# Last token group: one VectorE instruction moved behind the next tile's sum, and a third one moved to the second layer

## The chip, the core and the metric

The kernel runs on one core of one Trainium2 chip. The core has a matrix engine (TensorE, in the profile PE, with its weight loads as PEld), VectorE (DVE), ScalarE (ACT), GpSimd (POOL) and SyncE (SP, which here issues most of the transfers). The engines run side by side. Each takes its own instructions in order, and waits for others by semaphores. The metric is the device time of one execution in microseconds, less is better. Single executions are compared by their profile, kernels by the median of several runs.

## The reference

Two blocks follow one another: a gated linear attention (B = 4, H = 8 heads, S = 768 steps, 48 columns each), and a mixture of four two-layer networks over its output.

```python
for t in range(S):
    state = alpha[:, :, t, :, None] * state + einsum('bhd,bhe->bhde', k[:, :, t], v[:, :, t])
    y[:, :, t] = einsum('bhd,bhde->bhe', q[:, :, t], state)
x = y.transpose(0, 2, 1, 3).reshape(3072, 384)
p = domain_probs / (domain_probs.sum(-1, keepdims=True) + 1e-09)
for e in range(4):
    h = maximum(x @ w1[e], 0.0)                 # 3072 x 1024
    out += p[:, e:e + 1] * (h @ w2[e])          # 3072 x 384
```

## The kernel before, in words

**Tiling.** The sequence is cut into 24 units of 128 tokens (6 chunks of 4 batches). They form seven groups, `gi` = 0 to 6: the first and the last have 2 units (256 tokens), the others 4 (512 tokens). `LAST` is 6. For each group and each expert `e`, `up` makes the first layer, 8 tiles of hidden columns (`fc` = 0 to 7, each 128 hidden columns by the group's tokens), and `down` makes the second. Groups 5 and 6 take turns: (5, 0), (6, 0), (5, 1), (6, 1) and so on, so that they share weights. Attention for a later group runs between the matrix products of earlier ones: `deal` gives its steps due times from fixed costs, and `advance` emits the steps that are due. Attention is over before group 5 begins.

**Three parts.** A float32 operand is written as three fp32r parts: top, low and dif, in the text also top, L and D. The products of the parts then run on TensorE in the fast format. In the first layer a tile has six products into a PSUM buffer `one` and three into a buffer `two`. These and the second layer's sums `ops0`, `ops1` share four PSUM buffers (tag "g").

**A tile's way (groups 2 to 6, where `split2` holds).** ScalarE copies `one` to `t` with a factor (L538). VectorE adds `two` to `t` (L540). Then `hidden_parts`, a generator, makes the hidden tile's parts: ScalarE the top part with the ReLU (L563), VectorE the low part L as max(t, 0) - top (L565), and VectorE the D part from top and L (`make_dif`, L573). `hidden_parts` makes D only for the first half of the tokens. The other half goes into the queue `later`, which `down` empties, one piece at every fifth product (`n % 5 == 4`). `t` has two buffers.

**Order by hand.** Everything is emitted in program order, and each engine keeps that order. `up` appends the generator of tile k to `finish`, and runs it to its end after the products of tile k+1 have been emitted and before tile k+1's own copy and add. So VectorE's order is add(k), L(k), D(k), add(k+1), and ScalarE's is t(k), top(k), t(k+1). After the last tile of a stage (`fc` = 7) its generator is run at once.

**Second layer.** `down` takes two slots (units) at a time. A pass has 48 products: parts 0 and 1 (top and low) of `fc` 0 to 5 for both slots (n = 0 to 23), parts 0 and 1 of `fc` 6 and 7 (n = 24 to 31), and part 2 (D) of all `fc`, for the first slot n = 32 to 39, for the second n = 40 to 47. `add_up` adds a finished sum into `acc` on VectorE (L641; in the last group the tile's name is QT), with `p_fine` for `ops0` after n = 29 (first slot) and n = 31 (second), with `p_all` for `ops1` after n = 39 and n = 47. For expert 0 the first of them is a copy on ScalarE (L639). A group of four units has two passes, and the second reuses the PSUM buffers of the first. A group of two has one pass.

Of the kernel before, what the change touches and what calls it, by code (L numbers as in the profile page):

```python
# [20 lines left out]
def kernel(  # L21
# [49 lines left out]
    NT = B * P  # L71
# [11 lines left out]
    n = np.arange(QUAD)[None, :]  # L83
# [30 lines left out]
    LAST = len(groups) - 1  # L114
# [22 lines left out]
    finish = deque()  # L137
# [4 lines left out]
    later = deque()  # L142
# [91 lines left out]
    def background():  # L234


        for piece in list(splitting):
            if next(piece, splitting) is splitting:
                splitting.remove(piece)
        if making and len(splitting) < 4:  # L240
            splitting.append(making.popleft())
            next(splitting[-1])
# [225 lines left out]
    def x_part(gi, part, kc):  # L468
        n = len(groups[gi]) * P
        if gi < LAST:  # L470
            return xTs[gi][:, part, kc, :n]
        t, i = divmod(part * KC + kc, NP * P // n)
        return xTs[gi][t].rearrange("p a n -> p (a n)")[:, i * n:(i + 1) * n]
# [20 lines left out]
    def up(gi, e, fc, slots=None):  # L494
        n = len(groups[gi]) * P
        lo, hi = (slots.start * P, slots.stop * P) if slots else (0, n)
        begins, ends = lo == 0, hi == n
        c, f = divmod(fc, FPQ)
        i = first_piece(gi, e) + c
        if fc == 0 and begins:  # L500
            for k in range(NQ):
                hidden[k] = hid.tile([P, 3, FPQ, NT], F32R, name="hT", bufs=NQ)
        if fc in ((0, 2) if gi == 1 else (0,)) and begins and not split2(gi, e):
            half = range(fc, fc + 2) if gi == 1 else range(NQ)
            for k in half:
                load_piece(1, (gi * E + e) * NQ + k, beside=True)
        if makes[0](gi, e) and ends and fc in SPLIT_AT[e in (0, E - 1)]:
            k = SPLIT_AT[e in (0, E - 1)].index(fc)
            making.append(split_piece(0, (gi * E + e) * NQ + k))
        if gi == 0 and ends and e + 1 < E and fc == (0 if e == 0 else FCH // 2):  # L510
            for k in range(NQ):
                load_piece(0, (e + 1) * NQ + k)
        col = slice(f * P, (f + 1) * P)
        if split1(gi, e):
            w = wt[0][i].rearrange("p t (c f) -> p t c f", f=QF)[:, :, :, col]
        else:
            w = wt[0][i].rearrange("p (c f) -> p c f", f=QF)[:, :, col]
        parts = [hidden[c][:, part, f, lo:hi] for part in range(3)]
        whole = parts[2].bitcast(F32)
        one = ps.tile([P, NT], F32, name="one", tag="g", bufs=4)[:, :hi - lo]  # L520
        if not split1(gi, e):
            for kc in range(KC):
                nc.tensor.matmul(one, lhsT=w[:, kc], rhs=xraws[gi][:, kc, lo:hi],  # L523
                                 start=(kc == 0), stop=(kc == KC - 1))
            nc.scalar.activation(out=whole, in_=one, func=ACT.Relu)
        else:
            two = ps.tile([P, NT], F32, name="two", tag="g", bufs=4)[:, :n]
            for out, terms in ((one, (1, 0)), (two, (2,))):
                for part in terms:
                    for kc in range(KC):  # L530
                        nc.tensor.matmul(out, lhsT=w[:, part, kc], rhs=x_part(gi, part, kc),  # L531
                                         start=(part == terms[0] and kc == 0),
                                         stop=(part == terms[-1] and kc == KC - 1))
            while finish:
                for _ in finish.popleft():
                    pass
            t = work.tile([P, NT], F32, name="t")[:, :n]
            nc.scalar.activation(out=t, in_=one, func=ACT.Copy, scale=FINE)  # L538
            if split2(gi, e):
                nc.vector.tensor_add(t, t, two)  # L540
                finish.append(hidden_parts(t, parts))
            else:
                nc.vector.tensor_add(whole, t, two)  # L543
                finish.append(rectified(whole))
        while finish and fc == FCH - 1:
            for _ in finish.popleft():
                pass
        background()
        if f == FPQ - 1 and ends:
            if gi == 0:  # L550
                for k in range(AHEAD if i == E * NQ - 1 else 0):
                    load_piece(0, i + 1 + k)
            elif gi != LAST - 1:
                del wt[0][i]
                load_piece(0, i + AHEAD)
            while late:
                load_piece(1, late.popleft())
            while stores:
                stores.popleft()()

    def hidden_parts(x, parts):
        top, low, dif = parts
        nc.scalar.activation(out=top, in_=x, func=ACT.Relu, scale=TRIM)  # L563
        yield
        nc.vector.scalar_tensor_tensor(out=low, in0=x, scalar=0.0, in1=top.bitcast(F32),  # L565
                                       op0=ALU.max, op1=ALU.subtract)

        n = x.shape[-1]
        make_dif(*(part[:, :n // 2] for part in parts))
        later.append([part[:, n // 2:] for part in parts])  # L570

    def make_dif(top, low, dif):
        nc.vector.scalar_tensor_tensor(out=dif, in0=top.bitcast(F32), scalar=1 / 4096.0,  # L573
                                       in1=low.bitcast(F32), op0=ALU.mult, op1=ALU.subtract)

    def rectified(t):
        nc.scalar.activation(out=t, in_=t, func=ACT.Relu)
        yield

    def down(gi, e, slots, between):  # L580


        first = first_piece(gi, e)
        halves_ = split2(gi, e)
        if slots[0] == 0 and makes[1](gi, e):
            making.extend(split_piece(1, first + k) for k in range(NQ))
        if slots[0] == 0 and makes[0](gi, e) and 0 < e < E - 1:
            making.extend(split_piece(0, first + k) for k in range(2, NQ))
        sums = [[ps.tile([P, DM], F32, name=f"ops{j}", tag="g", bufs=4)
                 for j in range(2 if halves_ else 1)] for _ in slots]  # L590

        kinds = [((0, 1), range(FCH - 2)), ((0, 1), range(FCH - 2, FCH)), ((2,), range(FCH))]
        steps = [(part, i, fc) for parts, tiles in (kinds if halves_ else [((3,), range(FCH))])
                 for part in parts for i in range(len(slots)) for fc in tiles]
        for n, (part, i, fc) in enumerate(steps):
            c, f = divmod(fc, FPQ)
            h = hidden[c][:, :, f, slots[i] * P:(slots[i] + 1) * P]
            advance(cost(1, gi, e) / FCH / (3 if halves_ else 1))
            while between and n >= between[0][0] * len(steps):
                between.popleft()[1]()  # L600
            if n == len(steps) // 2:
                background()
            if later and n % 5 == 4:
                make_dif(*later.popleft())
            if halves_:
                w = wt[1][first + c].rearrange("p t (c d) -> p t c d", d=DM)[:, part, f]
                nc.tensor.matmul(sums[i][part // 2], lhsT=h[:, part], rhs=w,  # L607
                                 start=(fc == 0 and part != 1), stop=(fc == FCH - 1 and part != 0))
            else:
                w = wt[1][first + c].rearrange("p (c d) -> p c d", d=DM)[:, f]  # L610
                nc.tensor.matmul(sums[i][0], lhsT=h[:, 2].bitcast(F32), rhs=w,  # L611
                                 start=(fc == 0), stop=(fc == FCH - 1))
            if part >= 1 and fc == FCH - 1:
                add_up(gi, e, slots[i], part // 2, sums[i][part // 2 if halves_ else 0])
        while between:
            between.popleft()[1]()
        background()
        if slots[-1] == len(groups[gi]) - 1 and gi != LAST - 1:
            while makes[1](gi, e) and (making or splitting):
                background()  # L620

            for c in range(NQ):
                del wt[1][first + c]
                if c < NQ // 2 or gi == LAST:
                    load_piece(1, first + NQ + c)
                else:
                    late.append(first + NQ + c)
# [68 lines left out]
    with tc.manual_schedule():  # L696
# [48 lines left out]
        for (gi, e), after in zip(tasks, [*tasks[1:], (None, None)]):  # L745
# [6 lines left out]
            for k, slots in enumerate(turns):  # L752

                between = deque()
                if after[1] == 0:
                    for step, at in enumerate((0.0, 0.52, 0.62, 0.72)):
                        at = at * len(turns) - k
# [33 lines left out]
```

## Time and profile before

| | us |
|---|---|
| median of 9 runs (1083.57 to 1085.19) | 1084.7 |
| the profiled execution, its own time | 1083.78 |
| its span in the profile | 1082.0 |
| PE busy | 1057.0 (98%) |
| PEld busy | 899.0 (83%) |
| DVE busy | 779.3 (72%) |
| ACT busy | 563.8 (52%) |
| POOL busy | 32.8 (3%) |

The page's times are of one execution. "L607 PE MATMUL ops<-w,hT" is an instruction of line 607 on PE that writes `ops` and reads `w` and `hT`; "x6" is a count. In a timeline the first column is the start in us and the second the length. What stands in brackets is how long the engine sat idle before it, and what ended that. In the chain that ended last, the second column is the time that the piece took on the chain. TensorE's clock was granted in full in nearly every slice, 0.998 in the mean.

### The profile page before, as it was taken

How to read it: one execution, taken by the hardware profiler on the slowest of the kernel's cores; microseconds unless marked ns; L12 is line 12 of the kernel's file. 1: busy time of each engine (PE TensorE's matmuls, PEld its weight loads, DVE VectorE, ACT ScalarE, POOL GpSimd, SP SyncE). 2: the span in 40 equal slices, each digit the busy share in tenths (PEclk: the TensorE clock that was granted, in tenths of full speed). 3: DMA queues.
4: the chain of work that ended last, by engine and by line, in shares of the span. 5: the costliest groups of instructions: out<-in, count | busy, mean ns of one | idle time of the engine just before them, and what ended most of it. 6: DMA issues, size and time to landing. Idle time of an engine off the chain costs nothing.

```text
span 1082.0 us, 21627 instructions
## 1 busy us (share of the span) xinstructions
PE 1057.0 (98%) x8460; PEld 899.0 (83%) x8460; DVE 779.3 (72%) x1743; ACT 563.8 (52%) x1202; POOL 32.8 (3%) x71
## 2 busy tenths in 40 slices
PE   8889899999999999999999999999999999999998
PEld 8766677686776798898898898898988989898987
DVE  5578777647567869778878777986787965756565
ACT  5786776674746555436546436565464442323232
POOL 2000000000000100000000000000000000000000
PEclk9999999999999999999999999999999999999999
DMA  8597689886696967757759559577594444453530
GB/s 123 156 329 229 213 267 374 297 307 237 220 320 217 407 201 268 283 169 294 269 167 353 216 172 361 182 254 273 147 348 190 176 191 175 175 186 164 206 160 30
DMA packets 158838, 251.67 MB, mean 233 GB/s; under 512 B 120112, under 2 KB 135344, under 8 KB 136208
## 3 DMA queue, kind: packets, MB, share of 16 engines
q1 hardware_dynamic: 149600, 208.82, 56.0%
q0 software_dynamic: 5760, 41.29, 9.7%
q8 instruction: 67, 1.10, 0.4%
q10 hardware_dynamic: 3376, 0.17, 0.3%
q14 instruction: 35, 0.29, 0.1%
HBM read 207.79 MB, written 42.47 MB: 231 GB/s over the span
## 4 chain that ended last, share of the span: by engine, by line
PE 77%; DVE 9%; ACT 7%; DMA 4%; issue 2%; SPq 1%; ACTq 0%; DVEq 0%
PE ops L607 25%; PE one L531 19%; PE two L531 9%; PE ops L611 9%; PE sc L333 5%; PE yps L425 3%; PE tp L265 2%; ACT qb L307 2%; DVE t L540 2%; DVE hT L565 2%; PE one L523 2%; ACT hT L563 2%; PE sps L454 1%; PE far L388 1%; DMA w<-kept 1%
## 5 line engine op out<-in xcount | busy, mean ns | idle before, releaser
L607 PE MATMUL ops<-w,hT 128*128 128x384 f32 x1728 | 318.5, 340 | 1.9 <-DVE acc L641 1.4
L607 PEld LDWEIGHTS ops<-w,hT 128*128 128x128 f32 x1728 | 299.2, 188 | 7.4 <-DVE acc L641 2.7
L531 PE MATMUL one<-xT,w 128*128 128x512 f32 x960 | 253.9, 400 | 1.1 <-DMA w<-kept 0.9
L531 PEld LDWEIGHTS one<-xT,w 128*128 128x128 f32 x960 | 175.8, 188 | 42.6 <-issue 2.4
L538 ACT ACTIVATE t<-one 128x512 f32<-128x512 f32 (+1 forms) x192 | 106.0, 552 | 162.7 <-PE one L531 146.5
L307 ACT COPY qb<-QT 64x256 f32<-64x256 f32 x336 | 136.5, 406 | 70.0 <-DVE QT L288 35.5
L563 ACT ACTIVATE hT<-t 128x512 fp32r<-128x512 f32 (+1 forms) x160 | 94.3, 590 | 122.3 <-DVE t L540 121.2
L565 DVE SCALAR_TENSOR_TENSOR hT<-t,hT 128x512 fp32r<-128x512 f32 (+1 forms) x160 | 102.2, 638 | 75.5 <-ACT hT L563 74.1
L531 PE MATMUL two<-xT,w 128*128 128x512 f32 x480 | 136.3, 392 | 0.0
L611 PE MATMUL ops<-hT 128*128 128x384 f32 x384 | 134.4, 493 | 0.0
L573 DVE SCALAR_TENSOR_TENSOR hT<-hT 128x256 fp32r<-128x256 f32 (+1 forms) x320 | 117.4, 395 | 5.5
L540 DVE TENSOR_TENSOR t<-t,two 128x512 f32<-128x512 f32 (+1 forms) x160 | 100.6, 629 | 23.7 <-PE two L531 13.2
L531 PEld LDWEIGHTS two<-xT,w 128*128 128x128 f32 x480 | 90.2, 188 | 19.9
L611 PEld LDWEIGHTS ops<-hT 128*128 128x128 f32 x384 | 69.5, 191 | 40.0 <-issue 0.8
L343 DVE COPY_PREDICATED near<-masks,sc 128x256 f32<-128x256 uint8 x144 | 77.0, 535 | 18.0 <-PE sc L333 14.9
L314 DVE TENSOR_TENSOR QT<-QT,dec 128x256 f32<-128x256 f32 x144 | 60.6, 421 | 32.6 <-ACT qb L307 32.2
L333 PEld LDWEIGHTS sc<-qb,KT 128*64 128x64 f32 x2304 | 72.8, 138 | 9.2 <-issue 7.1
L333 PE MATMUL sc<-qb,KT 128*64 128x64 f32 x2304 | 77.0, 224 | 0.2 <-ACT qb L307 0.2
L641 DVE SCALAR_TENSOR_TENSOR acc<-ops,p_all,acc 128x384 f32<-128x384 f32 x82 | 49.4, 612 | 29.2 <-PE ops L607 13.8
L325 ACT COPY KT<-KT 128x256 f32<-128x256 f32 x144 | 59.8, 415 | 3.1
L326 DVE TENSOR_TENSOR KT<-KT,dec 128x256 f32<-128x256 f32 x144 | 60.2, 418 | 1.5 <-PE tp L265 1.3
L543 DVE TENSOR_TENSOR hT<-t,two 128x512 f32<-128x512 f32 x32 | 22.0, 687 | 35.6 <-ACT t L538 25.3
(88 smaller groups left out, 970.7 us busy)
## 6 DMA issues: line engine op xcount, KB each, us to landing
w<-kept SPq DMA_DIRECT2D x144, 1152.0 KB
kept<-w POOLq DMA_DIRECT2D x32, 1152.0 KB, 7.6
hT<-in_moe_w_dram SPq DMA_DIRECT2D x32, 384.0 KB
w<-in_moe_w_dram SPq DMA_DIRECT2D x48, 128.0 KB
ra<-in_alpha_dram SPq DMA_DIRECT2D x23, 192.0 KB
rk<-in_k_dram SPq DMA_DIRECT2D x23, 192.0 KB
rq<-in_q_dram SPq DMA_DIRECT2D x23, 192.0 KB
out_dram<-acc POOLq DMA_DIRECT2D x18, 192.0 KB, 5.9
```

What stands on the lines that cost most here:

```text
L307: nc.scalar.copy(out=qb[rows, :, i, :].rearrange("p a (b r) -> p a b r", r=m), in_=qv[rows])
L314: nc.vector.tensor_mul(qv, qv, spread(dv[:, :, :, 0], m))
L333: nc.tensor.matmul(out[HALF * s:HALF * (s + 1), 2 * p:2 * p + 2, :], lhsT=KTs[li][:, p, HALF * s:HALF * (s + 1)], rhs=qbs[li][:, p, :, QUA ...
L343: nc.vector.copy_predicated(near.rearrange("p a (b two r) -> p a b two r", two=2, r=m)[:, :, :, 1, :], mk.unsqueeze(1).broadcast_to([P, H, ...
L531: nc.tensor.matmul(out, lhsT=w[:, part, kc], rhs=x_part(gi, part, kc), start=(part == terms[0] and kc == 0), stop=(part == terms[-1] and k ...
L538: nc.scalar.activation(out=t, in_=one, func=ACT.Copy, scale=FINE)
L540: nc.vector.tensor_add(t, t, two)
L563: nc.scalar.activation(out=top, in_=x, func=ACT.Relu, scale=TRIM)
L565: nc.vector.scalar_tensor_tensor(out=low, in0=x, scalar=0.0, in1=top.bitcast(F32), op0=ALU.max, op1=ALU.subtract)
L573: nc.vector.scalar_tensor_tensor(out=dif, in0=top.bitcast(F32), scalar=1 / 4096.0, in1=low.bitcast(F32), op0=ALU.mult, op1=ALU.subtract)
L607: nc.tensor.matmul(sums[i][part // 2], lhsT=h[:, part], rhs=w, start=(fc == 0 and part != 1), stop=(fc == FCH - 1 and part != 0))
L611: nc.tensor.matmul(sums[i][0], lhsT=h[:, 2].bitcast(F32), rhs=w, start=(fc == 0), stop=(fc == FCH - 1))
```

## The change

Three edits, all in order and place; each product, part and sum stays.

- In the last group, `finish`'s generator is only run by its first step (the top part) before the next tile's copy. Its second step (L) is run after that tile's add. In the other groups all is as before.
- `hidden_parts` makes no D in the first layer if the tile is narrower than 512 tokens, which is the last group. All 256 tokens of a tile go into `later` as one piece, so a pass has eight pieces of 128x256 where eight of 128x128 were left.
- `down` takes a piece from `later` at every fourth product (`n % 4 == 3`), in all groups that have pieces, 2 to 6: at n = 3, 7, ... 31, where it was n = 4, 9, ... 39.

```diff
-            while finish:
-                for _ in finish.popleft():
+            ends_first = gi < LAST
+            for steps in finish:
+                for _ in steps if ends_first else [next(steps)]:
                     pass
+            ahead = [] if ends_first else list(finish)
+            finish.clear()
             t = work.tile([P, NT], F32, name="t")[:, :n]
             nc.scalar.activation(out=t, in_=one, func=ACT.Copy, scale=FINE)
             if split2(gi, e):
                 nc.vector.tensor_add(t, t, two)
+                for steps in ahead:
+                    next(steps, None)
                 finish.append(hidden_parts(t, parts))
...
         n = x.shape[-1]
-        make_dif(*(part[:, :n // 2] for part in parts))
-        later.append([part[:, n // 2:] for part in parts])
+        at = n // 2 if n == NT else 0
+        if at:
+            make_dif(*(part[:, :at] for part in parts))
+        later.append([part[:, at:] for part in parts])
...
-            if later and n % 5 == 4:
+            if later and n % 4 == 3:
                 make_dif(*later.popleft())
```

## The prediction, made before the changed kernel was run

> **What bounds the kernel now.** I read the page's busy shares first, then the chain that ended last over 990 to 1082 us, then the timeline of the stage that the change names, then the waits.
>
> ```profile
> PE 1057.0 (98%) x8460; PEld 899.0 (83%) x8460; DVE 779.3 (72%) x1743; ACT 563.8 (52%) x1202; POOL 32.8 (3%) x71
> ```
>
> TensorE is the bound as an average: after 140 us nearly every slice is full. But the chain leaves PE in one kind of place, the first layer of the last group (tiles of 128x256). Its periods repeat like this one (start, length, what):
>
> ```profile
> 1013.73 0.02 issue
> 1013.75 0.04 DVE hT L573
> 1013.78 0.17 issue
> 1013.96 0.42 DVE t L540
> 1014.38 0.02 issue
> 1014.41 0.43 ACT hT L563
> 1014.83 0.02 issue
> 1014.86 0.44 DVE hT L565
> ```
>
> One period runs from add to add, 1012.39 to 1013.96: 1.57 us. VectorE adds (L540), ScalarE makes the top part (L563), VectorE makes L (L565) and then D (L573), and only behind these, in VectorE's order, comes the next add. PE's side of it, and ScalarE's, in the timeline:
>
> ```profile
> 1012.02 0.98 PE L531 MATMUL one<-KT,w 128*128 128x256 f32 x6
> ...
> 1012.86 0.62 PE L531 MATMUL two<-KT,w 128*128 128x256 f32 x3
> 1013.16 0.37 ACT L538 ACTIVATE t<-one 128x256 f32<-128x256 f32 x1
> ...
> 1013.58 0.78 PEld L531 LDWEIGHTS one<-KT,w 128*128 128x128 f32 x6 [0.30 <-ACT t L538]
> ```
>
> The six products start 0.42 us after a copy `t` starts: they wait for the PSUM buffer that it empties (four buffers, two per tile). Unhindered, at the start of the same stage (1006.00, 1007.08, 1008.15, 1009.23), a tile takes PE 1.08 us. So the stage begins at PE's pace and ends at 1.57. From the first product of its first layer to the first of its second it lasts 10.41, 10.42, 10.72 and 10.41 us for the four experts (from 901.13, 953.56, 1006.00, 1059.12), where 8 x 1.08 = 8.64 would do. A busy PE row hides this: the waits are put half on PEld and half into longer matmuls.
>
> The other place that matters is the second layer of groups 2 to 4, where VectorE also does attention:
>
> ```profile
> 511.82 1.42 DVE L573 SCALAR_TENSOR_TENSOR hT<-hT 128x256 fp32r<-128x256 f32 x4
> 513.16 1.13 DVE L641 SCALAR_TENSOR_TENSOR acc<-ops,p_fine,acc 128x384 f32<-128x384 f32 x2
> 513.82 2.35 PE L607 MATMUL ops<-w,hT 128*128 128x384 f32 x12 [0.83 <-DVE acc L641]
> ...
> 682.36 1.49 PE L607 MATMUL ops<-w,hT 128*128 128x384 f32 x7 [0.58 <-DVE acc L641]
> ...
> 855.40 1.00 PEld L607 LDWEIGHTS ops<-w,hT 128*128 128x128 f32 x6 [0.39 <-DVE acc L641]
> ...
> 856.67 1.51 PEld L607 LDWEIGHTS ops<-w,hT 128*128 128x128 f32 x9 [0.27 <-DVE acc L641]
> ```
>
> There the second pair of slots waits until `acc` has emptied the first pair's sums, and `acc` stands behind D pieces in VectorE's queue.
>
> [...] D of 128x128 lasts 0.29 us, yet the next add starts 0.21 after it (1013.75 to 1013.96), and `t` starts 0.33 after a top part of 0.42. [...]
>
> **The change, part by part.**
>
> *L behind the next add (gi = 6 only).* Nothing is added; 32 L instructions trade places with 32 adds. New order: top(k-1), t(k) on ScalarE; add(k), L(k-1) on VectorE. A tile now has three loops:
> - PE: 1.08.
> - add to top 0.45 (0.43 + 0.02), top to next t 0.33, t to add 0.41 (0.37 + 0.04): 1.19.
> - `t` has two buffers, so t(k+1) waits for L(k-1), which is now behind add(k): add to L, L to t 0.45 (0.43 + 0.02), t to add 0.41. Add to L without a wait between them isn't in this trace; D to add overlaps by 0.08, so I take 0.42 - 0.08 = 0.34. Sum 1.20. Bounds: 0.30 (more overlap) to 0.45 (none, as where L follows a wait), sum 1.16 to 1.31.
>
> This wait through `t`'s buffers is what takes the place of the old one. Does 1.20 still hold PE up? With t(0) 0.97 after the first product (902.10 - 901.13), add(0) 0.41 later, top(0) 0.45 and t(1) 0.33 after that: t(1) at 2.16, t(2) at 3.35, then 1.20 each: t(6) at 8.15, t(7) at 9.35. The second layer's first product needs t(6) + 0.42 = 8.57, PE arrives at 8.64: no wait left. Its seventh product needs t(7) + 0.42 = 9.77 against 8.64 + 6 x 0.1735 = 9.68: 0.09. The same recurrence with the old order gives 10.43, where 10.41 was measured, so I trust it. At 1006 the first `t` came 0.3 late (1007.27); with that it gives 10.72 before (measured 10.72) and 8.88 after. Gain: 3 x (10.41 - 8.64) + (10.72 - 8.88) = 7.15. The 48 products behind it lose less too: they take 8.25, 8.25, 8.41, 8.26 to the last one's start, 47 x 0.1735 = 8.15 unhindered; I take 0.25 of these 0.57. Together **-7.4**. At 1.31 per tile t(6) + 0.42 is 9.01, and the gain falls by about 0.4 x 4 = 1.6.
>
> *All D in the second layer (gi = 6).* 64 D of 128x128 (0.288) become 32 of 128x256 (0.421). In the first layer 0.21 leaves VectorE's loop (that is in the sums above); in the second, 8 D of 0.34 start to start follow L(7). L(7) is at 10.66 after the stage's start (add(7) 9.76, top 10.21, then 0.45), so the seventh D ends at 13.5. Part 2 of the products begins at 8.64 + 32 x 0.1735 = 14.2: in time. The eighth D stands behind the first `acc`, which waits for product 29 and starts about 5.5 after the second layer's start (6.13 to its end, before); D then runs 6.05 to 6.47, and product 39 needs it at 6.77. Cover 0.3 us: **cost 0**, up to 0.3 x 4 if it slips by twice its cover.
>
> *One D per four products, not five (groups 2 to 6).* No instruction is added, no DMA and nothing on SP or POOL moves; loads of w follow PE's progress as before. What is queued behind a D: `acc`, and attention's steps. In program order of the changed kernel one more D stands ahead of slot 0's `acc` and two ahead of slot 1's: +0.34 and +0.67 us each time, in the first pass of each (group, expert); expert 0's first sums go through ScalarE and are spared. PE waits for these `acc` already three times: at 513.82 (+0.34), at 682.36 (+0.34), and at 855.40 and 856.67, where slot 1 sets the end (+0.67). Elsewhere cover exists: at 639.07 the `acc` ended 0.42 before PE came (638.04 + 0.61 = 638.65), at 1050.64 it was 0.75 (1049.28 + 0.61 = 1049.89), which shrinks to 0.08 and 0.41. Sum **+1.35**. Attention's steps come up to 0.34 later, but PE waited for ScalarE's attention copies (`lat`) only once for 0.9 us between 378 and 866 (the waits list), at 803, before a D is dealt: 0, bounds -0.5 (later ones have fewer D ahead) to +1.5.
>
> *Sum:* -7.4 + 1.35 = -6.05 on the profiled execution: span 1082.0 to 1076.0, its own time 1083.78 to 1077.7. That execution is 0.92 below the median of nine (1084.7); the same step from the median gives **1078.6**.
>
> **Rivals.**
> 1. *The buffer loop is slower than 1.20.* If each tile takes 1.45 (L held until the add is all done and the wait's cost on top), t(6) is at 3.35 + 4 x 1.45 = 9.15, the second layer starts at 9.57, and the gain is 4 x 0.84 + 0.25 - 1.35 = 2.3: 1082.4. For it: no add-L pair without a wait is in the trace. Against it: each other pair overlaps.
> 2. *The delayed `acc` costs nothing,* because attention's neighbours move with it: -7.4, 1077.3. For it: the later `acc` and steps have fewer D ahead. Against it: the three waits follow directly on runs of D.
> 3. *Slower.* D pieces dealt earlier push `acc` and attention in all 12 first passes of groups 2 to 4, and TensorE, full there, can't make it up. Price per pass 0.67 for slot 1's `acc` plus 0.34 for an attention step that PE meets: 12 x 1.01 = 12.1, less 7.4: 1089.4. It decides from 7.4 / 12 = 0.62 per pass. Against it: PE is busy 485.3 of 488 us from 378 to 866, and covers of 0.4 us and more stand at the other passes.
> 4. *The edit does nothing:* excluded, the changed program has the order described.
>
> **How the numbers follow.** Forecast 0.70, rival 1 0.11, rival 2 0.13, rival 3 0.06. What a measurement of this kernel can tell from no change is 0.2%, 2.2 us: 1082.5 to 1086.9. The forecast and rival 2 lie wholly on the faster side; rival 1 straddles the edge, so half of it counts as the same; half of rival 3 stops short of slower. Faster 0.885, same 0.075, slower 0.04. Range: low end rival 2 with attention's -0.5, 1076.8; high end the forecast with the loop's +1.6, attention's +1.5 and some of the eighth D's bound, 1082.0.
>
> **What would show it.** Right: adds (L540's successor) 1.20 apart in the last group, the stage 8.6 to 8.9 us, no PEld wait for `t` in it; PE's waits for `acc` longer by 0.3 at the places of 513, 682, 855. Wrong: adds 1.3 or more apart, new PE waits for D or `acc` after 900, or idle PE between 378 and 866 above the present 2.7 us by more than 3.

## The result, and the profile after

The changed kernel takes 1080.12 us (median of 9 runs, 1079.41 to 1082.29) against 1084.67 for the kernel before (29 runs, 1082.89 to 1087.82): ratio 0.9961, 95% interval 0.9952 to 0.9969. That is 4.55 us less by the medians and 4.2 by the ratio, where 6.05 was forecast. The measured time lies inside the range (1076.8 to 1082.0) and 1.5 us above the predicted 1078.6.

The page's first lines of the changed kernel, and its chain that ended last:

```profile
span 1078.7 us, 21595 instructions
PE 1054.0 (98%) x8460; PEld 898.4 (83%) x8460; DVE 774.4 (72%) x1711; ACT 566.6 (53%) x1202; POOL 32.7 (3%) x71
...
PE 82%; DVE 8%; ACT 6%; issue 2%; DMA 1%; SPq 0%; ACTq 0%; DVEq 0%
```

The 32 missing VectorE instructions are the D halves that became whole ones. PE's share of the chain is 82%, where it was 77% (80% in a second profile of the changed kernel). In the last group's first layer it no longer leaves PE. This is its list of pieces there (start, length, what), one stage of the first layer with the tiles of 128x256:

```profile
1009.14 0.72 PE one L531 x6
1009.86 0.36 PE two L531 x3
1010.22 0.72 PE one L531 x6
1010.94 0.36 PE two L531 x3
1011.30 0.87 PE one L531 x6
1012.17 0.36 PE two L531 x3
1012.52 0.93 PE one L531 x6
1013.45 0.35 PE two L531 x3
1013.80 0.94 PE one L531 x6
```

The first tiles take PE 1.08 us, as before. The last three of this stage do not keep that: from 1012.52 to 1013.80 it is 1.28. A chain that stays on PE is not the same as PE at its pace. The six products are 0.93 long in it because their first weight load waits. The timeline of the same stage has the loop:

```profile
1011.16 0.42 DVE L544 TENSOR_TENSOR t<-t,two 128x256 f32<-128x256 f32 x1 [0.53 <-ACT t L542]
...
1011.50 0.42 DVE L571 SCALAR_TENSOR_TENSOR hT<-t,hT 128x256 fp32r<-128x256 f32 x1
1011.62 0.42 ACT L569 ACTIVATE hT<-t 128x256 fp32r<-128x256 f32 x1 [0.49 <-DVE t L544]
...
1012.03 0.39 ACT L542 ACTIVATE t<-one 128x256 f32<-128x256 f32 x1
1012.45 0.42 DVE L544 TENSOR_TENSOR t<-t,two 128x256 f32<-128x256 f32 x1 [0.53 <-ACT t L542]
1012.47 0.65 PEld L531 LDWEIGHTS one<-KT,w 128*128 128x128 f32 x5 [0.15 <-ACT t L542]
```

Add to L is 0.34, as assumed. L to the next copy `t` is 0.53, not 0.45. Copy to add is 0.42. Together 1.29 between adds (1011.16 to 1012.45), and PE still waits 0.15 for `t`. Between L's end and the copy runs a separate wait instruction in ScalarE's queue. The kernel before has it too, but shorter (in ns: least, median, most). After, then before:

```profile
L542 ACTq EVENT_SEMAPHORE  x6: 38/38/38, 1009.4 to 1015.8; - x6
```

```profile
L538 ACTq EVENT_SEMAPHORE  x6: 17/17/17, 1008.1 to 1016.0; - x6
```

In groups 2 to 4 the waits for `acc` have grown (timelines at the prediction's three places):

```profile
515.77 1.49 PE L615 MATMUL ops<-w,hT 128*128 128x384 f32 x7 [1.16 <-DVE acc L649]
```

```profile
684.72 1.49 PE L615 MATMUL ops<-w,hT 128*128 128x384 f32 x7 [0.92 <-DVE acc L649]
```

```profile
857.71 1.00 PEld L615 LDWEIGHTS ops<-w,hT 128*128 128x128 f32 x6 [0.75 <-DVE acc L649]
...
859.32 1.85 PEld L615 LDWEIGHTS ops<-w,hT 128*128 128x128 f32 x11 [0.61 <-DVE acc L649]
```

0.83 became 1.16, 0.58 became 0.92, 0.39 became 0.75 and 0.27 became 0.61: a third of a microsecond each.

PE executes the same 8460 products in the same order in both kernels, so that starts can be compared one by one. Read from the traces:

| | before | after | difference |
|---|---|---|---|
| start to first second-layer product of group 2 | 378.50 | 380.13 | +1.63 |
| from there to the same of group 5 | 505.86 | 506.87 | +1.01 |
| from there to the last product's start | 193.43 | 187.53 | -5.90 |
| the four stages of the last group's first layer | 10.42, 10.43, 10.72, 10.41 | 9.02, 9.02, 9.31, 9.03 | -5.60 |

The first row has nothing to do with the change, which begins at group 2. The windows view shows where it arose (window, length, busy time and count of PE, PEld, DVE, ACT, POOL, then granted TensorE clock, DMA share, GB/s). First the changed kernel, then the kernel before:

```profile
124.00:128.00 4.00, 3.54 (x51) 2.55 (x52) 2.02 (x7) 2.80 (x7) 0.53 (x1) 0.65 0.85 332
```

```profile
124.00:128.00 4.00, 3.64 (x58) 2.70 (x58) 2.51 (x8) 2.86 (x8) 0.51 (x1) 1.00 0.85 334
```

The granted clock is 0.65 in the mean here and 0.93 in the next 4 us, and 0.50 from 126 to 128. That makes 3.4 us at half TensorE clock in the changed kernel's profiled execution, besides a stretch like it at 81 us that both have (0.50 from 82 to 84 in both). Without the first row, the two profiles differ by 4.9 us, not by the spans' 3.3. Such a stretch comes and goes from execution to execution (see the end).

### The profile page after: what moved, and what is told of

It reads as the page before. It is cut to its first block, busy times and chain, and to the rows that moved or that the text cites. A ratio compares the mean times of both kernels' runs of the same rounds, so it can differ in the third digit from the quotient of the medians.

```text
span 1078.7 us, 21595 instructions
## 1 busy us (share of the span) xinstructions
PE 1054.0 (98%) x8460; PEld 898.4 (83%) x8460; DVE 774.4 (72%) x1711; ACT 566.6 (53%) x1202; POOL 32.7 (3%) x71
## 4 chain that ended last, share of the span: by engine, by line
PE 82%; DVE 8%; ACT 6%; issue 2%; DMA 1%; SPq 0%; ACTq 0%; DVEq 0%
PE ops L615 26%; PE one L531 21%; PE two L531 10%; PE ops L619 9%; PE sc L333 5%; PE yps L425 3%; PE tp L265 3%; PE one L523 2%; ACT qb L307 2%; PE sps L454 2%; DVE near L343 1%; DVE hT L571 1%; PE far L388 1%; DVE t L544 1%; ACT hT L569 1%
## 5 line engine op out<-in xcount | busy, mean ns | idle before, releaser
L581 DVE SCALAR_TENSOR_TENSOR hT<-hT 128x256 fp32r<-128x256 f32 x288 | 112.0, 421 | 4.4
```

## Experiments

The first four were timed beside the kernel before on one chip, the other four on another. The kernel before took 1085.16 us on the first and 1084.18 on the second. Each diff is against the changed kernel, with three exceptions: edits 2 and 3 alone are shown against the kernel before, and one per six against both mends. A gain in the trace is the difference of two profiles. "Groups 2 to 4" is the stretch of the table's second row, "the end" that of its third.

**Edit 1 alone: L behind the next add.**

```diff
-        at = n // 2 if n == NT else 0
-        if at:
-            make_dif(*(part[:, :at] for part in parts))
+        at = n // 2
+        make_dif(*(part[:, :at] for part in parts))
...
-            if later and n % 4 == 3:
+            if later and n % 5 == 4:
```

> Only L is moved behind the next add; half of D stays in the first layer, and pieces go one per five products as before. Theory A (the gain is L's and D's removal from in front of the add, and what limits the last group now is the copy t, which waits for L through t's two buffers): VectorE has add to L 0.34, L to D 0.46, D to add 0.21, sum 1.01, so D in the first layer is covered, adds stay 1.29 apart as in the changed kernel, the four stages are 9.0 to 9.3 us as there, and the 1.0 us lost in groups 2 to 4 is not lost: 5.9 us under the kernel before, about 1078.8. Theory B (D's removal carries the gain): adds 1.4 or more apart, 3 us or less under the kernel before.

Measured: 1080.1 us against 1085.16, ratio 0.9960 (0.9946 to 0.9973). Adds 1.29 apart, stages 9.03, 9.03, 9.30, 9.03; groups 2 to 4 505.82, the end 187.36. Theory A holds in each number of the trace; by the medians the gain is 5.1, not 5.9 (its one execution at a mean clock of 0.998 is 6.1 under those of the kernel before, in the median; edit 3 alone, below, says why this is compared). Behind the add, D costs nothing in the first layer (timeline):

```profile
1010.86 0.42 DVE L544 TENSOR_TENSOR t<-t,two 128x256 f32<-128x256 f32 x1 [0.20 <-ACT t L542]
...
1011.20 0.42 DVE L571 SCALAR_TENSOR_TENSOR hT<-t,hT 128x256 fp32r<-128x256 f32 x1
1011.32 0.42 ACT L569 ACTIVATE hT<-t 128x256 fp32r<-128x256 f32 x1 [0.49 <-DVE t L544]
...
1011.65 0.29 DVE L580 SCALAR_TENSOR_TENSOR hT<-hT 128x128 fp32r<-128x128 f32 x1
...
1012.15 0.42 DVE L544 TENSOR_TENSOR t<-t,two 128x256 f32<-128x256 f32 x1 [0.21 <-ACT t L542]
```

VectorE, with D (L580), still idles 0.21 before the next add. The changed kernel's stages are the same within 0.02. So beside edit 1, edits 2 and 3 bring nothing to the last group.

**Edit 2 alone: D in the second layer.** L stays ahead of the add; pieces come one per four products in the last group, one per five elsewhere.

```diff
-        make_dif(*(part[:, :n // 2] for part in parts))
-        later.append([part[:, n // 2:] for part in parts])
+        at = n // 2 if n == NT else 0
+        if at:
+            make_dif(*(part[:, :at] for part in parts))
+        later.append([part[:, at:] for part in parts])
...
-            if later and n % 5 == 4:
+            if later and (n % 4 == 3 if gi == LAST else n % 5 == 4):
```

> Only the D parts of the last group go to the second layer (there one per four products; other groups one per five as before); L stays ahead of the next add. Theory A: add to top 0.45, top to L 0.45, L to add 0.34 without a wait between them: adds 1.24 apart, even a little less than the 1.29 of the changed kernel, stages about 8.8 us, 6.5 us under the kernel before, about 1078.2; moving L would then not be needed. Theory B (moving L is what counts): only D's 0.21 to 0.3 goes, adds 1.3 to 1.36 apart, 4 to 5.5 us under the kernel before.

Measured: 1077.9 us, ratio 0.9937 (0.9925 to 0.9950). Adds 1.24 apart, stages 8.79, 8.80, 9.08, 8.80; groups 2 to 4 505.62, the end 186.78: theory A. The simpler edit gives shorter stages than the whole change. The rhythm in the last group is not what did it: edit 3 alone, below, has the same rhythm there and leaves the stages at 10.41 to 10.70. L is back on the add's path, but without D behind it the next add can follow L at once (timeline):

```profile
1010.66 0.41 DVE L540 TENSOR_TENSOR t<-t,two 128x256 f32<-128x256 f32 x1
1011.11 0.42 ACT L563 ACTIVATE hT<-t 128x256 fp32r<-128x256 f32 x1 [0.55 <-DVE t L540]
...
1011.43 0.37 ACT L538 ACTIVATE t<-one 128x256 f32<-128x256 f32 x1
1011.56 0.43 DVE L565 SCALAR_TENSOR_TENSOR hT<-t,hT 128x256 fp32r<-128x256 f32 x1 [0.49 <-ACT hT L563]
...
1011.90 0.41 DVE L540 TENSOR_TENSOR t<-t,two 128x256 f32<-128x256 f32 x1
```

Add to top 0.45, top to L 0.45, L to add 0.34: 1.24. The copy `t` starts 0.32 after the top part and is not the limit. From L to the next add it is 0.34 without D; with D it was 0.67, since D reads what L wrote and starts 0.46 after L, and the add comes 0.21 later.

**Edit 3 alone: one piece per four products.**

```diff
-            if later and n % 5 == 4:
+            if later and n % 4 == 3:
```

> Only the rhythm of the D pieces is changed, to one per four products in all groups. Theory A: TensorE waits for acc 0.33 longer at two first passes of groups 2 to 4 and 0.68 longer at a third, part of it given back: 0.7 to 1.0 us slower than the kernel before, about 1085.5; adds of the last group 1.57 apart as before. Theory B (harmless, the shift of 1.0 in the one profile is chance): the same time as the kernel before within 0.3 us.

Measured: 1085.46 against 1085.16 us, ratio 1.0004 (0.9996 to 1.0012). The medians alone exclude neither theory. But they mix executions with mean clocks from 0.994 to 0.998, and stretches of half TensorE clock lower the mean (last section). A second stretch of 3.4 us in 1085 takes another 0.0016 off it, and each of the seven profiled executions with a mean of 0.998 had only one. So I compare the executions with this mean. Five executions of this kernel have 0.998, and took 1084.22 to 1084.54; five of the kernel before took 1082.74 to 1083.95. They do not overlap, and their medians are 0.80 apart. The trace agrees: groups 2 to 4 take 506.70, 0.84 more than before. This is theory A. In that stretch the waits list puts PEld's waits for `acc` as follows; first this kernel, then edit 1 alone with its one per five:

```profile
PEld ops L607 <- DVE acc L641: 4.1, 4, 1.5
```

```profile
PEld ops L614 <- DVE acc L648: 2.8, 4, 1.2
```

1.3 us more in the same four waits (total, times, longest; 2.7 in the kernel before). The changed kernel and the next one, with one per four too, have 4.1 as well. The last group is as before: adds 1.57 apart.

**Four buffers for `t` in the last group.** The changed kernel, with `t` cut out of the same 512 wide tiles:

```diff
-            t = work.tile([P, NT], F32, name="t")[:, :n]
+            if gi < LAST or fc % 2 == 0:
+                pair_t[0] = work.tile([P, NT], F32, name="t")
+            t = pair_t[0][:, :n] if gi < LAST else pair_t[0][:, fc % 2 * n:(fc % 2 + 1) * n]
```

> The changed kernel, but in the last group a tile's t is half of a 512 wide tile, so that t has four buffers in place of two and t(k+1) no longer waits for L(k-1). Theory A (the wait through t's buffers sets 1.29): adds 1.19 apart (0.45 + 0.33 + 0.41), stages 8.65 to 8.9 us, 1.2 us under the changed kernel, about 1078.9. Theory B (ScalarE's own order sets it, t starts 0.42 after the top part whatever VectorE does): adds 1.28 apart, the same time as the changed kernel.

Measured: 1078.29 us, ratio 0.9936 (0.9924 to 0.9949). Adds 1.18 apart, stages 8.62, 8.64, 8.62, 8.64: PE's own 8 x 1.08. The end takes 185.73, 1.8 less than in the changed kernel; groups 2 to 4 506.69, as there. The copy, freed of L, starts 0.32 after the top part (timeline):

```profile
1010.81 0.42 DVE L547 TENSOR_TENSOR t<-t,two 128x256 f32<-128x256 f32 x1 [0.42 <-ACT t L545]
...
1011.15 0.42 DVE L574 SCALAR_TENSOR_TENSOR hT<-t,hT 128x256 fp32r<-128x256 f32 x1
1011.27 0.42 ACT L572 ACTIVATE hT<-t 128x256 fp32r<-128x256 f32 x1 [0.49 <-DVE t L547]
1011.59 0.37 ACT L545 ACTIVATE t<-one 128x256 f32<-128x256 f32 x1
1011.99 0.42 DVE L547 TENSOR_TENSOR t<-t,two 128x256 f32<-128x256 f32 x1 [0.42 <-ACT t L545]
```

So the wait through `t`'s two buffers was the limit. It gave way at once when it was taken away, and theory B falls. The gain in the stages was above the 1.2 forecast for it: 1.86.

**One per five outside the last group, one per four in it.**

```diff
-            if later and n % 4 == 3:
+            if later and (n % 4 == 3 if gi == LAST else n % 5 == 4):
```

> The changed kernel, with the pieces of groups 2 to 5 again one per five products and only those of the last group one per four. Theory A (the rhythm costs 0.8 to 1.0 us in groups 2 to 4): from the first fp32r product of the second layer of group 2 to that of group 5 505.8 us as in the kernel before (506.9 in the changed kernel), the last group's stages 9.02 as in the changed kernel; 1.0 us under the changed kernel. Theory B (the 0.8 to 1.0 is a chance of placement, not the rhythm): 506.7 or more in this stretch, no gain.

Measured: 1079.53 against 1084.18 us, ratio 0.9958 (0.9945 to 0.9970). Groups 2 to 4 take 505.84, PEld's waits for `acc` 2.8 (2.7 in the kernel before), the stages 9.03 to 9.32. The trace is theory A's. The median is not below the changed kernel's on the same chip (1079.27, below): 1 us is less than the intervals' width. At a mean clock of 0.998 there is one execution, 1078.12, where the changed kernel has 1078.66 to 1079.9.

This kernel is also edit 2 alone with edit 1 added, so the two profiles price edit 1 on top of edit 2: the stages were 8.79, 8.80, 9.08, 8.80, and are now 9.03, 9.05, 9.32, 9.04. With two buffers for `t`, moving L as well as D cost 1.0 us.

**Both mends together:** four buffers and one per five.

> Both mends together: four t buffers in the last group, and one piece per five products outside it. If the two costs are independent: stages 8.63 us, 505.8 us in groups 2 to 4, 7.7 us under the kernel before and 2.5 under the changed kernel, about 1077.3. If mending one uncovers another wait: less than 2 us under the changed kernel.

Measured: 1077.51 us, ratio 0.9937 (0.9925 to 0.9949). Stages 8.62, 8.62, 8.62, 8.64, groups 2 to 4 505.91, the end 185.60: 7.8 us less than before in the two stretches together. No new wait came up in either stretch: in the trace the costs are independent. By the medians the gain on the changed kernel on the same chip is 1.8, less than the 2.5 forecast. But all five executions of that one had a mean clock of 0.998, and only two of this one: these took 1076.02 and 1076.13, 3.2 less than the changed kernel's median.

**One per six outside the last group,** else the same:

```diff
-            if later and (n % 4 == 3 if gi == LAST else n % 5 == 4):
+            if later and (n % 4 == 3 if gi == LAST else n % 6 == 5):
```

> As the kernel with both mends, but outside the last group one piece per six products, so that one D fewer stands ahead of slot 0's acc than in the kernel before. Theory A (acc behind D sets TensorE's wait): the waits for acc in groups 2 to 4 shrink by about 0.3 each, 505.1 to 505.4 us in the stretch, about 0.5 us under one per five. Theory B (the later D pieces delay the p_all sums and with them the next first layer by as much): no change against one per five, or up to 0.5 us slower.

Measured: 1076.12 us, ratio 0.9932 (0.9918 to 0.9945), 8.1 us under the kernel before by the medians. It is the lowest median, but its interval overlaps that of one per five, and at a mean clock of 0.998 it is only 0.2 lower (1075.86 against 1076.08). Groups 2 to 4 take 505.52, 0.4 less than with one per five and outside the 505.1 to 505.4 of theory A. Both theories have a part (the waits list of that stretch):

```profile
PEld ops L618 <- DVE acc L652: 1.7, 3, 0.8
PEld one L532 <- DVE acc L652: 1.3, 2, 0.8
```

Waits of the second pass's sums fell from 2.7 (one per five, both mends) to 1.7, and waits of the next first layer rose from 0.6 to 1.3.

**The changed kernel again.**

> The changed kernel once more, beside the others on one chip, to separate its own cost from chance: its first profile had two stretches of 3.4 us at half TensorE clock (81 and 125 us) where the kernel before had one, worth 1.6 us of its span. If that is chance, its median stays 4.5 to 5 us under the kernel before, and about 1 us above the one with one per five outside the last group.

Measured: 1079.27 against 1084.18 us, ratio 0.9956 (0.9944 to 0.9969). Its profile has one half-clock stretch in the first 130 us, and a span of 1078.1; groups 2 to 4 take 507.05, the end 187.87, close to the first profile's. The 1 us to one per five shows in the trace (507.05 against 505.84), not in the medians. So the first profile's 1.6 us was chance, and the 1.0 us was not.

## Why the prediction was right, and where its sizes were off

- *Where the loss sat, and that it would go:* right. The last group's first layer lost its 1.57, and the gain of the end, 5.9, is the whole of the change's gain.
- *L behind the add, size:* the term that was mis-sized. Forecast 7.15 for the stages, measured 5.60. The mechanism, a wait for L through `t`'s two buffers, was right. Of the loop's three terms add to L (0.34) and copy to add (0.41, measured 0.42) held. L to copy was taken as 0.45 (0.43 for L and 0.02 for the wait, as from add to top in the kernel before), and measured 0.53. The copy now waits for three semaphores (VectorE's, PE's and its own engine's). Two of these waits sit in the separate wait instruction ahead of it. In the kernel before this instruction has one wait and runs about 0.3 us ahead of the copy. Here it begins 0.03 after L's end and takes 38 ns, and the copy begins 0.045 after its end. So each of the five loops from t(1) on came 0.09 late: t(6) at 8.59 and not at 8.15. The second layer starts 0.43 after it, at 9.02, where PE arrives at 8.64. So 0.38 is lost in each of three stages, and 0.43 in the one whose first `t` comes late (9.31 for 8.88). The loop of 1.29 lies inside the stated 1.16 to 1.31. The four-buffer run shows the same term from the other side: without this wait the stages are 8.62 to 8.64 and the end is 7.7 shorter, where 7.4 was forecast.
- *The second layer's products behind the stage,* forecast 0.25 shorter: no. 47 intervals took 8.25, 8.26, 8.40, 8.26, as before. With four buffers they take 8.21 to 8.31, so the wait for L does not explain it. What holds them above 8.15 (47 x 0.1735, where 0.173 and 0.174 are the commonest distances between their starts) was not tried. For scale: a float32 product of the same 128x384, in groups 0 and 1 (L611), is two matmuls that start 0.32 apart.
- *All D in the second layer at no cost:* right. No wait for D appears. In the last stage the eighth piece runs from 6.04 to 6.46 after the second layer's start, as computed, and product 39 comes at 6.87. What the prediction did not see: this edit alone would have done (1.24), and beside the moved L it is idle.
- *One per four products, +1.35:* the mechanism and the places were right, each wait +0.33 to +0.36. The sum in the trace was +1.01 (+0.84 for the edit alone), because 0.33 came back at 693 us. There the next first layer waits for a buffer that the second pass's first `p_fine` sum empties. In both orders all eight pieces are done ahead of this sum, and VectorE works without a pause (no gap above 0.06 us in the 17 us before it), so the sum came no later. PE, which came 0.33 later, waited 0.2 for it and not 0.5.
- *Sum:* forecast -6.05, in the two stretches -4.9. The misses partly cancel, and that is luck. The stages gave 1.55 less than forecast and the products behind them 0.25 less. The rhythm cost 0.34 less, and 0.3 was gained in group 5's second layer. That last part was chance: the changed kernel's second profile gains nothing there.
- *Its signs:* the longer waits for `acc` came. Adds 1.20 apart, stages of 8.6 to 8.9 and no wait for `t` did not (1.29, 9.02 to 9.31, 0.15). The signs of being wrong did not come either, the first by a hair: 1.29 and not 1.3 between adds, no wait of PE for D or `acc` after 900, and 3.8 us of idle PE between 378 and 866.
- *Rivals.* A slower buffer loop (rival 1) was half true: 1.29, not 1.45. A harmless rhythm (rival 2) is refuted by the traces and by edit 3 alone. The slower outcome (rival 3) did not come, the covers at the other first passes held. By the halves that it names, the chances should have been 0.085 for the same and 0.03 for slower.

## What to carry to other kernels

When an instruction is put behind the next tile's work in a queue, its buffers are held one tile longer (adds 1.29 us apart with two buffers for `t`, 1.18 with four). Count the buffers it reads before pricing the new loop, and look for a separate wait instruction that the new wait puts on the path: here L's end to the copy took 0.115 us, where 0.02 was assumed.

Of a chain of two instructions where the second reads the first's result, moving the second off the path can be enough, since the first then overlaps what follows (L lasts 0.43 us, and the next add starts 0.34 after it). Here it gave more than moving the first (8.8 against 9.03 us for a stage) as long as `t` had two buffers; both moved, with four buffers, gave the most (8.63). L alone with four buffers was not tried.

When background pieces are dealt more densely, look for the sums queued behind them: here one third of a microsecond per place, on TensorE, which was busy for 485.3 of the 488 us from 378 to 866 in the kernel before.

## What the runs showed that I had not expected

Besides the very end of the span, TensorE's granted clock fell to 0.50 for stretches of 3.4 us at about 81 us, or between 123 and 129. Of the ten profiled executions three (the changed kernel's first, one per five outside the last group, and both mends together) had both stretches, at mean clocks of 0.996, 0.996 and 0.997, the others one, at 0.998. In the comparison above the second stretch costs 1.6 us of span, more than edit 3 is worth. What sets it off was not tried. From 120 to 124 PE was nearly idle in both profiles of that comparison (busy 0.94 and 0.86 us of 4), so this idle time alone doesn't tell which execution gets it. Comparing the starts of the same product in two traces, stretch by stretch, takes it out of the account, and so does comparing executions with the same mean clock.
